# Attention scores in blocks of 128 queries of one expert, on two halves of TensorE's rows

## Chip, cores and metric

One core of a Trainium2 chip runs the whole kernel. The metric is the device time of one execution in microseconds, median of three runs.

## The reference

A linear attention feeds a mixture of experts with ordinary causal attention (batch B = 8, S = 576 positions, eight heads or 512 features, E = 4 experts of width 64, the best two of four per position). Cut to the second part, in which the change lies:

```python
q = x @ wq[e]; k = x @ wk[e]; v = x @ wv[e]        # for each expert e
scores = scale * (q @ k.transpose(0, 2, 1))
scores = np.where(causal, -1000000000.0, scores)
scores = scores - scores.max(-1, keepdims=True)
a = np.exp(scores)
a /= a.sum(-1, keepdims=True) + 1e-09
ye = a @ v @ wo[e]
...
out += mask[..., None] * w[:, :, kk:kk + 1] * ye
```

## The kernel before, in words

The linear attention runs over 32 pairs of heads: K and Q projections, features, sums over keys, numerator and denominator. Four pairs make the input x of one batch. For each of the eight batches the experts are taken in two groups g of two experts, and a group passes through these steps:

- `proj_t`: Q and K of both experts, transposed (64 dims of one expert on rows 0 to 63, of the other on rows 64 to 127). Values are held as a high and a low F32R part; a product is three matmuls (high by high, high by low, low by high).
- `scores(g)`: nine blocks i of 64 queries. `evac_q` lays Q out as block diagonals of 128 x 128, so that one matmul over all 128 rows gives 64 queries of the one expert on PSUM rows 0 to 63 and the same queries of the other below. Block i sees 64 (i + 1) keys; block 8 is cut into 256 and 320. That makes 10 PSUM tiles and 30 matmuls.
- `soft`: for each tile DVE adds the causal mask to the last 64 columns and takes the row maximum, ACT takes the exponential into `a` with its row sum, and the tile is free.
- `stream_t`: DVE turns the row sums into factors with the gates, DVE or ACT scales the nine blocks of `a`, PE transposes 25 pieces of 128 x 128 in seven PSUM tiles, and `evac_t` copies them into `at`.
- `attend`: the product with V, then `evac_y`, and after the second group the output projection.

All PSUM is one pool of eight tiles of 128 x 512, shared by every step. A planner writes the program's order: each stream of steps has a position, and of the steps that could start within 100 ns of the earliest the one with the lowest position is put next, by a table of costs per instruction. `in_order` then fixes that order on each engine. A change of costs or of steps so moves instructions of other streams too, and decides which PSUM tile a step gets.

`half_mm` in the K and Q projections of the linear attention (L396) already places two matmuls of 64 rows on the two halves of the rows, in F32.

## Time and profile before

| | |
|---|---|
| median of 3 runs (lowest, highest) | 777.0 us (776.93, 779.72) |
| the profiled execution's own time, its span | 773.74 us, 771.6 us |
| PE, DVE, ACT, POOL busy | 95%, 67%, 62%, 27% of the span |
| mean granted TensorE clock | 0.989 |

Busy is the time in which an engine had at least one instruction in work; matmuls overlap one another, so the sum over groups is more than the busy time, and the pace of a run of matmuls is read from start to start in the timeline.

### The profile page before, as it was taken

The page shows a single profiled execution, that of the slowest core. Times are in us where ns is not written, and L with a number is a line of the kernel's source. Part 1 is how long each engine was busy: PE and PEld are TensorE (multiplying, and loading weights), DVE is VectorE, ACT ScalarE, POOL GpSimd, SP SyncE. Part 2 cuts the span into 40 slices and gives each one's busy share as a digit, 9 for nine tenths or more (in the row PEclk, how much of TensorE's full clock was granted, in tenths as well). Part 3 has the DMA queues.
Part 4 walks back from the last instruction along what each step waited for, and adds up shares of the span by engine and source line. Part 5 has one row for each costly group of instructions (what it writes and reads, how often), then busy time and mean ns, then how long its engine had stood idle before and what let it go on. Part 6 is the DMA issues. An engine that isn't in the chain of part 4 may idle for free.

```text
span 771.6 us, 17860 instructions
## 1 busy us (share of the span) xinstructions
PE 730.1 (95%) x6927; PEld 564.4 (73%) x6927; DVE 520.3 (67%) x1368; ACT 475.7 (62%) x1096; POOL 211.5 (27%) x208
## 2 busy tenths in 40 slices
PE   5979899889999899999999999999999999999997
PEld 4655567666788567977779767886678876887986
DVE  3986855796567766698558766578657785376572
ACT  2764655667567664768546756666666686476474
POOL 2533542132321334040350144213332343010000
PEclk9999999899999999999999999999999999999998
DMA  4442321102112022102121212120211211010011
GB/s 122 141 143 64 93 57 34 35 18 67 53 34 97 17 69 82 54 17 82 51 67 35 78 36 73 48 96 17 68 52 34 65 35 35 2 47 18 1 62 62
DMA packets 38756, 43.63 MB, mean 57 GB/s; under 512 B 19088, under 2 KB 21648, under 8 KB 38672
## 3 DMA queue, kind: packets, MB, share of 16 engines
q1 hardware_dynamic: 38672, 42.49, 18.5%
q8 instruction: 55, 0.90, 0.5%
q14 instruction: 29, 0.24, 0.1%
HBM read 32.58 MB, written 9.44 MB: 54 GB/s over the span
## 4 chain that ended last, share of the span: by engine, by line
PE 80%; DVE 9%; DMA 3%; issue 2%; ACT 2%; SPq 2%; POOL 1%; DVEq 0%; POOLq 0%; ACTq 0%
PE ps_c L225 39%; PE ps_c L543 8%; PE ps_c L396 7%; PE ps_c L798 6%; PE ps_c L449 6%; PE ps_c L829 6%; PE ps_c L534 4%; PE ps_c L457 4%; DVE a L788 3%; DMA v_in<-in_v_dram 2%; SPq L257 2%; PE ps_c L467 1%; POOL mx L505 1%; DVE sm L778 1%; DVE u L507 0%
## 5 line engine op out<-in xcount | busy, mean ns | idle before, releaser
L505 POOL PARTITION_ALL_REDUCE mx<-u x64 | 138.4, 2212 | 203.7 <-ACT u L234 163.5
L225 PE MATMUL ps_c<-xh,qk 128*128 128x320 f32 (+1 forms) x512 | 109.2, 300 | 0.0
L236 ACT ACTIVATE ek<-ek 128x1152 f32<-128x1152 f32 x64 | 74.7, 1167 | 20.9 <-DVE ek L431 20.4
L236 ACT ACTIVATE a<-ps_c,nm 128x256 f32<-128x256 f32 (+7 forms) x160 | 79.7, 503 | 12.6 <-DVE nm L682 4.4
L225 PEld LDWEIGHTS ps_c<-xh,qk 128*128 128x128 f32 x512 | 83.4, 188 | 3.8 <-issue 1.9
L575 POOL PARTITION_BROADCAST xf<-dr x32 | 28.3, 884 | 188.1 <-DMA dr<-dc 59.5
L798 PE MATMUL ps_c<-ident,a 128*128 128x128 f32 x400 | 61.0, 295 | 17.9 <-DVE a L788 11.9
L225 PE MATMUL ps_c<-xl,qk 128*128 128x256 f32 (+1 forms) x256 | 75.5, 295 | 0.5 <-DVE xl L229 0.5
L682 DVE TENSOR_REDUCE nm<-ps_c 128x1 f32<-128x256 f32 (+7 forms) x160 | 71.8, 457 | 4.9
L798 PEld LDWEIGHTS ps_c<-ident,a 128*128 128x128 f32 x400 | 46.7, 148 | 36.3 <-DVE a L788 13.8
L449 PE MATMUL ps_c<-ek,v_in 128*64 128x256 f32 x512 | 63.0, 388 | 8.7 <-DMA v_in<-in_v_dram 6.6
L507 DVE TENSOR_TENSOR u<-u,mx 128x576 f32<-128x576 f32 x64 | 62.8, 992 | 10.2 <-POOL mx L505 9.9
L236 ACT ACTIVATE mx<-u 128x576 f32<-128x576 f32 x64 | 43.8, 684 | 41.3 <-DVE u L507 41.2
L431 DVE TENSOR_TENSOR ek<-ps_c,pmax 128x512 f32<-128x512 f32 (+1 forms) x96 | 50.3, 549 | 16.5 <-PE ps_c L457 16.3
L225 PE MATMUL ps_c<-vg,xh 128*128 128x260 f32 (+1 forms) x320 | 60.6, 289 | 0.0
L428 DVE TENSOR_REDUCE pmax<-ps_c 128x4 f32<-128x512 f32 (+1 forms) x96 | 49.9, 548 | 14.2 <-PE ps_c L396 14.2
L234 ACT COPY at<-ps_c 128x512 f32<-128x512 f32 (+1 forms) x94 | 49.2, 571 | 16.4 <-PE ps_c L798 14.9
L449 PEld LDWEIGHTS ps_c<-ek,v_in 128*64 128x64 f32 x512 | 35.3, 137 | 29.3 <-issue 4.6
L225 PE MATMUL ps_c<-yh,wo 128*128 128x256 f32 (+1 forms) x256 | 52.1, 298 | 0.0
L225 PE MATMUL ps_c<-kkh,qbdh 128*128 128x256 f32 (+7 forms) x160 | 51.0, 319 | 0.6 <-ACT a L236 0.6
L225 PEld LDWEIGHTS ps_c<-vg,xh 128*128 128x128 f32 (+1 forms) x320 | 47.2, 178 | 3.5 <-issue 2.0
L225 PE MATMUL ps_c<-kkl,qbdh 128*128 128x256 f32 (+7 forms) x160 | 49.7, 311 | 0.0
(119 smaller groups left out, 1635.8 us busy)
## 6 DMA issues: line engine op xcount, KB each, us to landing
v_in<-in_v_dram SPq DMA_DIRECT2D x32, 320.0 KB, 3.0
q_in<-in_qt_dram SPq DMA_DIRECT2D x64, 144.0 KB, 2.9
out_dram<-ot SPq DMA_DIRECT2D x32, 288.0 KB, 2.1
k_in<-in_kt_dram SPq DMA_DIRECT2D x32, 160.0 KB, 2.9
k_in<-in_kt_dram SPq DMA_DIRECT2D x32, 128.0 KB, 2.9
dc<-dr SPq DMA_DIRECT2D x128, 2.2 KB, 1.9
ot<-in_wts_dram SPq DMA_DIRECT2D x5, 288.0 KB, 3.6
k_in<-in_kt_dram SPq DMA_DIRECT2D x32, 32.0 KB, 2.4
```

The source lines that it names most:

```text
L225: nc.tensor.matmul(o, a, b, start=start, stop=stop, skip_group_check=True)
L234: nc.scalar.copy(o, i)
L236: nc.scalar.activation(o, i, func, **kw)
L396: nc.tensor.matmul(o, a, b, start=True, stop=True, skip_group_check=True)
L428: dve(n * 128, [mk], [pk]).tensor_reduce(out=m[:, us], in_=src, axis=AX.X, op=ALU.max, apply_absolute_value=True)
L431: dve(n * 128, [f'ek{p % EKB}1'], [pk, mk]).tensor_tensor(out=ek2[p % EKB][:, 1, us, :], in0=src, in1=m[:, us].unsqueeze(2).to_broadcast([ ...
L449: nc.tensor.matmul(o[64 * h:64 * h + 64], v_in[:, 4 * h + t, :], ek[:, :, 4 * h + t, :], start=t == 0, stop=False, skip_group_check=True)
L505: nc.gpsimd.partition_all_reduce(M, U, 128, bass_isa.ReduceOp.absmax)
L507: dve(S, [uk], [mk]).tensor_tensor(out=U, in0=U, in1=M, op=ALU.subtract)
L543: nc.tensor.matmul(ps[64 * h:64 * h + 64, 0:n], kvi[:, c, 64 * h:64 * h + 64], P_[h][c][:, s0:s1], start=c == 0, stop=c == 1, skip_group_c ...
L682: dve(n, [('nm', g, c)], [pk]).tensor_reduce(out=nm[g][:, c:c + 1], in_=src, axis=AX.X, op=ALU.max, negate=True)
L798: nc.tensor.transpose(ps[:, k * 128:(k + 1) * 128], a_blk[i][:, j, :], ident)
```

## The change

Queries 0 to 511 are taken in four blocks of 128 queries of one expert. The two experts of a group form a pair of matmuls of 64 rows, one on each half of the rows, which write two PSUM tiles; product by product the pair alternates. Block 8, the last 64 queries, keeps the block diagonal of both experts. There are still ten tiles and 30 matmuls in a step, 24 of them of 64 rows. `evac_q` writes the first 512 queries straight (128 rows at once) and only the last 64 as diagonals. The mask of blocks 0 to 7 is 128 columns wide. The factors of the sums are made in two instructions, the first eight with the gates as they lie on DVE, the ninth with a copy that POOL makes. `at` is laid out by expert, and a PSUM tile of transposes takes the pieces that lie together there, first blocks 0, 2, 4 and 6. The planner's costs for F32 and F32R matmuls change as well (`RATE`, `LDW`); positions and order tables stay.

```diff
+RATE = 2.18
+LDW = 109.0
...
         elif a.dtype == F32R:
-            cost = max(n / 2.4, 107.0) + 2.5
+            cost = max(n / RATE, LDW) + 5
...
-    maskf = xf[:, 0:128]
-    nc.gpsimd.memset(maskf, 0.0)
-    nc.gpsimd.affine_select(out=maskf, in_=maskf, pattern=[[-1, 128]], compare_op=ALU.is_ge,
+    mask2 = sb("mask2", [128, 128])
+    nc.gpsimd.memset(mask2, 0.0)
...
-    a_sets = [[sb(f"a{x}{i}", [128, (i + 2) // 2, 128]) for i in range(NB)] for x in range(AB)]
-    at = sb("at", [128, 25, 128])
-    qbd2 = [[sb(f"qbd{p}{g}", [128, NB, 128], F32R) for p in "hl"] for g in range(QB)]
+    a_sets = [[sb(f"a{x}{c}", [128, c // 2 + 1, 128]) for c in range(9)] for x in range(AB)]
+    at = sb("at", [128, 2, NJ, S])
+
+    q2 = [[sb(f"q{p}{g}", [128, S - 64], F32R) for p in "hl"] for g in range(QB)]
+    qbd2 = [[sb(f"qbd{p}{g}", [128, 128], F32R) for p in "hl"] for g in range(QB)]
...
         def evac_q(g, s0, s1, pk, ps):
-            i0, i1 = s0 // 64, s1 // 64
-            for h in range(2):
-                r = slice(64 * h, 64 * h + 64)
-                src = ps[r, 0:s1 - s0].rearrange("p (i s) -> p i s", s=64)
-                hi, lo = (qbd2[g % QB][x][r, i0:i1, r] for x in range(2))
-                hk = ('qbdh', g, s0, h)
+            pieces = [(min(s1, 512) - s0, slice(0, 128), [t[:, s0:min(s1, 512)] for t in q2[g % QB]], 0, f'q{g % QB}')]
+            if s1 == S:
+                for e in range(2):
+                    r = slice(64 * e, 64 * e + 64)
+                    pieces.append((64, r, [t[r, r] for t in qbd2[g % QB]], 512 - s0, f'qbd{g % QB}'))
+            for k, (n, r, (hi, lo), o, key) in enumerate(pieces):
+                src, hk = ps[r, o:o + n], ('qhi', g, s0, k)
                 yield Step('ACT', [pk], hot=True)
-                act(s1 - s0, hi, src, [hk, f'qbd0{g % QB}'], [pk], scale=SCALE)
+                act(n, hi, src, [hk, f'{key}0'], [pk], scale=SCALE)
                 yield Step('DVE', [hk], hot=True)
-                dve(s1 - s0, [f'qbd1{g % QB}'], [hk, pk]).scalar_tensor_tensor(
+                dve(n, [f'{key}1'], [hk, pk]).scalar_tensor_tensor(
                     out=lo, in0=src, scalar=SCALE, in1=hi.bitcast(F32), op0=ALU.mult, op1=ALU.subtract)
             plan.release('c', (pk, ps))
...
-            for i in range(NB):
-                w = 64 * (i + 1)
-                for s0, s1 in ((0, w),) if i < 8 else PARTS:
-                    pk, ps = yield Step('PE', [f'qbd0{g % QB}', f'qbd1{g % QB}', f'kk0{g % QB}', f'kk1{g % QB}'], 'c', ready), pos[0] + SLOPE[2] * i / 9
-                    o = ps[:, 0:s1 - s0]
-                    for n, (q_, k_) in enumerate(((0, 0), (0, 1), (1, 0))):
-                        mm(o, qbd2[g % QB][q_][:, i, :], kk2[g % QB][k_][:, s0:s1], n == 0, n == 2, s1 - s0, pk,
-                           [f'qbd{q_}{g % QB}', f'kk{k_}{g % QB}'])
-                    plan.spawn(soft(g, i, s0, s1, pk, ps), pos[0])
+            Q, K, x = q2[g % QB], kk2[g % QB], g % QB
+            products = ((0, 0), (0, 1), (1, 0))
+            need = [f'q0{x}', f'q1{x}', f'kk0{x}', f'kk1{x}']
+            for i in range(4):
+
+                w = 128 * (i + 1)
+                t0 = yield Step('PE', need, 'c', ready), pos[0] + SLOPE[2] * i / 5
+                t1 = yield Step('PE', need, 'c'), pos[0] + SLOPE[2] * i / 5
+                for n, (q_, k_) in enumerate(products):
+                    for e, (pk, ps) in enumerate((t0, t1)):
+                        r = slice(64 * e, 64 * e + 64)
+                        plan.run('PE', max(w / RATE, LDW) / 2 + 8, [pk], need)
+                        nc.tensor.matmul(ps[:, 0:w], Q[q_][r, 128 * i:128 * i + 128], K[k_][r, 0:w],
+                                         start=n == 0, stop=n == 2, skip_group_check=True)
+                for e, (pk, ps) in enumerate((t0, t1)):
+                    plan.spawn(soft(g, 2 * i + e, 0, w, pk, ps), pos[0])
+            need = [f'qbd0{x}', f'qbd1{x}', f'kk0{x}', f'kk1{x}']
+            for s0, s1 in PARTS:
+                pk, ps = yield Step('PE', need, 'c', ready), pos[0] + SLOPE[2] * 4 / 5
+                for n, (q_, k_) in enumerate(products):
+                    mm(ps[:, 0:s1 - s0], qbd2[x][q_], K[k_][:, s0:s1], n == 0, n == 2, s1 - s0, pk, need)
+                plan.spawn(soft(g, 8, s0, s1, pk, ps), pos[0])
...
-            if s1 == 64 * (i + 1):
-                dve(64, [pk], []).tensor_tensor(out=ps[:, n - 64:n], in0=ps[:, n - 64:n], in1=mask, op=ALU.add)
+            if i < 8 or s1 == S:
+                m = mask2 if i < 8 else mask
+                d = m.free_size()
+                dve(d, [pk], []).tensor_tensor(out=ps[:, n - d:n], in0=ps[:, n - d:n], in1=m, op=ALU.add)
...
-        yield Step('DVE', ['lg'], pred=lambda: all(('v', b, j) in done for j in range(NJ)))
+        yield Step('DVE', ['lg'], pred=lambda: all(('v', b, j) in done for j in range(NJ)) and (not b or ('n', b - 1, 1) in done))
...
-        yield Step('POOL', [G], pred=has('n', b - 1, 1) if b else None)
-        for g in range(2):
+        yield Step('POOL', [G])
+        for e in range(2):
+            plan.run('POOL', 200, ['gb'], [G])
+            nc.gpsimd.tensor_copy(gb[64 * e:64 * e + 64, :], w[0:64, 4, e:4:2])
+        done.add(('gate', b))
+
+
+    def at_groups():
+        out = []
+        for j in (0, 1):
             for e in range(2):
-                for h in range(2):
-                    plan.run('POOL', 130, ['gb'], [G])
-                    nc.gpsimd.tensor_copy(gb[64 * e:64 * e + 64, g, h:NB:2],
-                                          w[64 * h:64 * h + 64, 0:5 - h, 2 * g + e])
-        done.add(('gate', b))
-
-    units = [(i, j) for j in range(NJ) for i in range(2 * j, NB)]
+                out.append(([(2 * i + e, j) for i in range(j, 4)], [(0, 512 - 128 * j, at[:, e, j, 128 * j:512], None)]))
+        out.append(([(2 * i + e, 2) for e in range(2) for i in (2, 3)], [(0, 512, at[:, :, 2, 256:512], "p (e s) -> p e s")]))
+        out.append(([(8, j) for j in range(4)], [(0, 512, at[:, :, 0:4, 512:S].rearrange("p e j s -> p j e s"), "p (j e s) -> p j e s")]))
+        out.append(([(6, 3), (7, 3), (8, 4)], [(0, 256, at[:, :, 3, 384:512], "p (e s) -> p e s"),
+                                               (256, 128, at[:, :, 4, 512:S], "p (e s) -> p e s")]))
+        return out
+
+    groups = at_groups()
+    AT = [('at', k) for k in range(len(groups))]
...
-                dve(9, sk, ['gb']).tensor_tensor(out=s_, in0=s_, in1=gb[:, g, :], op=ALU.mult)
+                dve(8, sk, ['gate']).tensor_tensor(out=s_[:, 0:8].rearrange("p (i e) -> p i e", e=2),
+                                                   in0=s_[:, 0:8].rearrange("p (i e) -> p i e", e=2),
+                                                   in1=gt[:, 3, 0:4, 2 * g:2 * g + 2], op=ALU.mult)
+                dve(1, sk, ['gb']).tensor_tensor(out=s_[:, 8:9], in0=s_[:, 8:9], in1=gb[:, g:g + 1], op=ALU.mult)
                 done.add(('n', b, g))
                 for i in range(NB):
-                    w = 64 * (i + 1)
+                    w = 128 * (i // 2 + 1) if i < 8 else S
...
-                for u0 in range(0, 25, 4):
-                    n = min(4, 25 - u0)
-                    kc, ps = yield Step('PE', [('a', x, units[u0 + k][0]) for k in range(n)], 'c',
-                                        has('av', last // 2, last % 2) if last >= 0 else None), pos + SLOPE[3] * u0 / 25
-                    for k in range(n):
-                        i, j = units[u0 + k]
-                        plan.run('PE', 107, [kc], [('a', x, i)])
-                        nc.tensor.transpose(ps[:, k * 128:(k + 1) * 128], a_blk[i][:, j, :], ident)
-                    plan.spawn(evac_t(u0, n, kc, ps, last, b, g), pos)
+                for k, (slots, goes) in enumerate(groups):
+                    kc, ps = yield Step('PE', [('a', x, c) for c, j in slots], 'c',
+                                        has('av', last // 2, last % 2) if last >= 0 else None), pos + SLOPE[3] * k / 7
+                    for n, (c, j) in enumerate(slots):
+                        plan.run('PE', LDW + 5, [kc], [('a', x, c)])
+                        nc.tensor.transpose(ps[:, n * 128:(n + 1) * 128], a_blk[c][:, j, :], ident)
+                    plan.spawn(evac_t(k, goes, kc, ps, b, g), pos)
...
-    def evac_t(u0, n, kc, ps, last, b, g):
-        src = ps[:, 0:n * 128].rearrange("p (u c) -> p u c", c=128)
-        st = Step(copies(n * 128), [kc], hot=True)
+    def evac_t(k, goes, kc, ps, b, g):
+        st = Step(copies(sum(n for _, n, _, _ in goes)), [kc], hot=True)
         yield st
-        copy(st.eng, n * 128, at[:, u0:u0 + n, :], src, [('at', u0)], [kc])
+        for o, n, dst, shape in goes:
+            src = ps[:, o:o + n]
+            if shape:
+                src = src.rearrange(shape, **({'e': 2, 's': 64} if 'j' in shape else {'e': 2}))
+            copy(st.eng, n, dst, src, [('at', k)], [kc])
...
-        for i0_, i1 in ((0, 4), (4, 9)):
-            ak = [('at', x) for x in range(0, 25, 4)]
-            pk, ps = yield Step('PE', ak, 'c', ready), pos + SLOPE[3]
-            js = range(0, i1 // 2 + i1 % 2)
+                    and all(('at', b, g, k) in done for k in range(len(groups))))
+
+        for s0, s1 in PARTS:
+            pk, ps = yield Step('PE', AT, 'c', ready), pos + SLOPE[3]
+            js = range(0, (s1 + 127) // 128)
             for j in js:
                 kn = min(128, S - 128 * j)
-                i0 = max(i0_, 2 * j)
-                o, n = jbase(j) + i0 - 2 * j, 64 * (i1 - i0)
+                q0 = max(s0, 128 * j)
                 for e in range(2):
-                    plan.run('PE', 2 * n / 2.4 + 27, [pk], [f'vs{j}'] + ak)
-                    nc.tensor.matmul(ps[64 * e:64 * e + 64, 64 * (i0 - i0_):64 * (i1 - i0_)].rearrange("p (i s) -> p i s", s=64),
-                                     vs[j][:kn, g, e, :], at[:kn, o:o + i1 - i0, 64 * e:64 * e + 64],
+                    plan.run('PE', 2 * (s1 - q0) / RATE + 5, [pk], [f'vs{j}'] + AT)
+                    nc.tensor.matmul(ps[64 * e:64 * e + 64, q0 - s0:s1 - s0], vs[j][:kn, g, e, :], at[:kn, e, j, q0:s1],
                                      start=j == 0, stop=j == js[-1], skip_group_check=True)
-            plan.spawn(evac_y(b, g, 64 * i0_, 64 * i1, pk, ps), pos)
+            plan.spawn(evac_y(b, g, s0, s1, pk, ps), pos)
```

On PE, second group of the second batch (index 1), first matmul of each tile or block, before; `ps_c_61` to `ps_c_68` are the eight PSUM tiles, `qbdh` the high part of the block diagonals, the last number the keys:

```order
L225 MATMUL ps_c_66<-kkh_151,qbdh_149 128x64
...
L225 MATMUL ps_c_64<-kkh_151,qbdh_149 128x128
...
L225 MATMUL ps_c_68<-kkh_151,qbdh_149 128x192
...
L225 MATMUL ps_c_63<-kkh_151,qbdh_149 128x256
...
L225 MATMUL ps_c_62<-kkh_151,qbdh_149 128x320
...
L225 MATMUL ps_c_67<-kkh_151,qbdh_149 128x384
...
L225 MATMUL ps_c_65<-kkh_151,qbdh_149 128x448
...
L225 MATMUL ps_c_61<-kkh_151,qbdh_149 128x512
...
L225 MATMUL ps_c_66<-kkh_151,qbdh_149 128x256
...
L225 MATMUL ps_c_64<-kkh_151,qbdh_149 128x320
```

The same place now; the two rows of a width are the two experts, `qh` is the high part of the queries laid out straight:

```order
L671 MATMUL ps_c_66<-kkh_154,qh_150 128x128
L671 MATMUL ps_c_68<-kkh_154,qh_150 128x128
...
L671 MATMUL ps_c_65<-kkh_154,qh_150 128x256
L671 MATMUL ps_c_67<-kkh_154,qh_150 128x256
...
L671 MATMUL ps_c_61<-kkh_154,qh_150 128x384
L671 MATMUL ps_c_66<-kkh_154,qh_150 128x384
...
L671 MATMUL ps_c_68<-kkh_154,qh_150 128x512
L671 MATMUL ps_c_65<-kkh_154,qh_150 128x512
...
L219 MATMUL ps_c_67<-kkh_154,qbdh_152 128x256
...
L219 MATMUL ps_c_61<-kkh_154,qbdh_152 128x320
```

Before, a tile of this step (66) comes back at the ninth tile; now 66 comes back at the sixth, and the 512-wide pair and block 8 take 68, 65, 67 and 61, the second to fifth, once more.

On PE a little later, where the transposes of this group begin, before (`ek` by `ones` are sums over keys of the linear attention, `a_139` to `a_147` the nine blocks of exponentials, `mx` by `kv` numerators):

```order
L457 MATMUL ps_c_68<-ek_100,ones 32x128 x16
L457 MATMUL ps_c_68<-ek_100,sel 32x128 x4
L798 MATMUL ps_c_66<-ident,a_139 128x128
L798 MATMUL ps_c_66<-ident,a_140 128x128
L798 MATMUL ps_c_66<-ident,a_141 128x128
L798 MATMUL ps_c_66<-ident,a_142 128x128
...
L543 MATMUL ps_c_67<-mx_123,kv_110 64x256
L543 MATMUL ps_c_67<-mx_124,kv_110 64x256
```

The same place now (`a_140` to `a_148` are the nine blocks, the last rows ahead of the transposes denominators):

```order
L452 MATMUL ps_c_65<-ek_101,ones 32x128 x16
L452 MATMUL ps_c_65<-ek_101,sel 32x128 x4
L538 MATMUL ps_c_66<-mx_124,kv_111 64x256
L538 MATMUL ps_c_66<-mx_125,kv_111 64x256
...
L529 MATMUL ps_c_68<-mx_121,kv_110 32x320
L529 MATMUL ps_c_68<-u_115,kv_110 32x320
L820 MATMUL ps_c_62<-ident,a_140 128x128
L820 MATMUL ps_c_62<-ident,a_142 128x128
L820 MATMUL ps_c_62<-ident,a_144 128x128
L820 MATMUL ps_c_62<-ident,a_146 128x128
```

Numerators and denominators now stand ahead of the transposes, not among them, and the first tile of transposes takes blocks 0, 2, 4, 6 where it took 0, 1, 2, 3.

On DVE, first group of the fourth batch (index 3), between the last copy of the gates' logits (`lg`) and softmax, before (`ge`, `gt`, `gs` belong to the gates, `nm` is the maximum):

```order
L568 RECIPROCAL dc_127<-dc_127 128x9
L652 COPY lg<-ps_c_64 64x4
L735 TENSOR_TENSOR ge<-lg 128x80
...
L744 TENSOR_TENSOR gt<-lg,gs 128x20
L681 TENSOR_TENSOR ps_c_65<-ps_c_65,mask 128x64
L682 TENSOR_REDUCE nm_163<-ps_c_65 128x1
L681 TENSOR_TENSOR ps_c_63<-ps_c_63,mask 128x64
```

The same place now:

```order
L692 TENSOR_TENSOR ps_c_68<-ps_c_68,mask_77 128x128
L693 TENSOR_REDUCE nm_166<-ps_c_68 128x1
...
L693 TENSOR_REDUCE nm_166<-ps_c_63 128x1
L692 TENSOR_TENSOR ps_c_64<-ps_c_64,mask 128x64
L693 TENSOR_REDUCE nm_166<-ps_c_64 128x1
...
L648 COPY lg<-ps_c_65 64x4
...
L746 TENSOR_TENSOR ge<-lg 128x80
L748 TENSOR_TENSOR ge<-ge,tri 128x80
```

The eight instructions of the gates stood ahead of the masks; now they stand behind all masks and maxima of the step, and so does the last copy of `lg`.

## Rows read from the trace of the kernel before

**Rows 1.** The page, parts 1 and 4: engines, and the chain by engine.

```profile
PE 730.1 (95%) x6927; PEld 564.4 (73%) x6927; DVE 520.3 (67%) x1368; ACT 475.7 (62%) x1096; POOL 211.5 (27%) x208
...
PE 80%; DVE 9%; DMA 3%; issue 2%; ACT 2%; SPq 2%; POOL 1%; DVEq 0%; POOLq 0%; ACTq 0%
```

**Rows 2.** Waits of PE over the span: us in total, times, longest us.

```profile
PE ps_c L798 <- DVE a L788: 11.9, 15, 2.3
```

**Rows 3.** Timeline of PE in one scores step: start us, us, what.

```profile
432.32 0.28 PE L225 MATMUL ps_c<-kkh,qbdh 128*128 128x64 f32 x1
...
432.65 0.31 PE L225 MATMUL ps_c<-kkh,qbdh 128*128 128x128 f32 x1
...
434.20 0.34 PE L225 MATMUL ps_c<-kkh,qbdh 128*128 128x384 f32 x1
...
434.74 0.37 PE L225 MATMUL ps_c<-kkh,qbdh 128*128 128x448 f32 x1
...
435.35 0.40 PE L225 MATMUL ps_c<-kkh,qbdh 128*128 128x512 f32 x1
...
436.06 0.27 PE L225 MATMUL ps_c<-kkh,qbdh 128*128 128x256 f32 x1
...
436.94 3.07 PE L829 MATMUL ps_c<-at,vs 128*64 128x256 f32 x28
```

**Rows 4.** Timeline of DVE over the same stretch.

```profile
433.14 0.23 DVE L681 TENSOR_TENSOR ps_c<-ps_c,mask 128x64 f32<-128x64 f32 x1
...
433.54 0.22 DVE L681 TENSOR_TENSOR ps_c<-ps_c,mask 128x64 f32<-128x64 f32 x1
...
434.54 0.22 DVE L681 TENSOR_TENSOR ps_c<-ps_c,mask 128x64 f32<-128x64 f32 x1
...
435.14 0.22 DVE L681 TENSOR_TENSOR ps_c<-ps_c,mask 128x64 f32<-128x64 f32 x1
...
443.24 5.23 DVE L788 TENSOR_SCALAR a<-a,sm 128x64 f32<-128x64 f32 x6
```

**Rows 5.** Timeline of ACT over the same stretch.

```profile
433.87 0.19 ACT L236 ACTIVATION_READ_ACCUMULATOR a<-ps_c,nm 128x1 f32 x1
...
435.63 0.19 ACT L236 ACTIVATION_READ_ACCUMULATOR a<-ps_c,nm 128x1 f32 x1
```

**Rows 6.** Chain that ended last, in order of time, 380 to 440 us.

```profile
381.38 2.09 PE ps_c L543 x16
383.47 1.11 PE ps_c L534 x16
...
394.36 1.09 PE ps_c L396 x16
395.45 0.42 PE ps_c L225 x2
```

**Rows 7.** Timeline of PE where a K projection begins.

```profile
393.84 0.40 PE L225 MATMUL ps_c<-vg,xh 128*128 128x260 f32 x2
394.08 0.28 PE L225 MATMUL ps_c<-vg,xl 128*128 128x260 f32 x1
394.29 1.16 PE L396 MATMUL ps_c<-wf,k_in 64*128 64x128 f32 x16
```

**Rows 8.** Groups on DVE, shapes apart: xcount | busy us, mean ns | idle.

```profile
L681 DVE TENSOR_TENSOR ps_c<-ps_c,mask 128x64 f32<-128x64 f32 x144 | 32.1, 223 | 0.7 <-PE ps_c L225 0.4 <-ACT at L234 0.4
...
L431 DVE TENSOR_TENSOR ek<-ps_c,pmax 128x128 f32<-128x128 f32 x32 | 9.1, 284 | 0.1
...
L775 DVE TENSOR_TENSOR sm<-sm 128x1 f32<-128x1 f32 x16 | 5.3, 330 | 0.9 <-ACT a L236 0.9
```

**Rows 9.** Timeline of PE at one group of transposes; in brackets idle time, releaser.

```profile
262.76 0.52 PE L798 MATMUL ps_c<-ident,a 128*128 128x128 f32 x3 [1.28 <-DVE a L788]
263.72 0.44 PE L798 MATMUL ps_c<-ident,a 128*128 128x128 f32 x2 [0.44 <-DVE a L788]
264.74 2.41 PE L798 MATMUL ps_c<-ident,a 128*128 128x128 f32 x11 [0.58 <-DVE a L788]
```

More of the change, by code (lines that the diff above doesn't have):

```diff
@@ L48 @@
 NPAIRS = B * NP
+RATE = 2.18
+LDW = 109.0
 PSUM_TILES = (("c", 8, 512),)
-def jbase(j):
-    return 10 * j - j * j
 def at_batch(b):
     return NP * b + BOFF[b]
-def abase(i):
-    return sum((ii + 2) // 2 for ii in range(i))
 class Step:
@@ L218, in mm @@
         if a.dtype == F32:
-            cost = max(n * 4 / 2.4, 214.0) + 2.5
+            cost = max(n * 4 / RATE, 2 * LDW) + 5
         elif a.dtype == F32R:
-            cost = max(n / 2.4, 107.0) + 2.5
+            cost = max(n / RATE, LDW) + 5
         else:
@@ L271, in tile_linear_attn_moe @@
         r_ = slice(64 * h, 64 * h + 64)
-        nc.vector.tensor_copy(mask[r_, :], maskf[r_, r_])
+        nc.vector.tensor_copy(mask[r_, :], mask2[r_, r_])
     tri = sb("tri", [128, 4, 4])
@@ L360, in zeros @@
         for x in range(AB):
-            for i in range(0, NB, 2):
-                yield Step('POOL')
-                plan.run('POOL', 88, [('a', x, i)])
-                nc.gpsimd.memset(a_sets[x][i][:, i // 2, 64:128], 0.0)
+            yield Step('POOL')
+            plan.run('POOL', 88, [('a', x, 8)])
+            nc.gpsimd.memset(a_sets[x][8][:, 4, 64:128], 0.0)
         done.add(('w', 4))
@@ L393, in half_mm @@
     def half_mm(o, a, b, n, w, r):
-        plan.run('PE', 2 * n / 2.4 + 20, [w], r)
+        plan.run('PE', 2 * n / RATE + 8, [w], r)
         nc.tensor.matmul(o, a, b, start=True, stop=True, skip_group_check=True)
@@ L532, in stream_n @@
                         g = 64 * h + 32 * c
[L533 removed]
+                        plan.run('PE', n / RATE + 5, [pk], Pk + [kvk])
                         nc.tensor.matmul(ps[g:g + 32, 0:n], kvi[:, 2, g:g + 32], P_[h][c][:, s0:s1],
```

13 lines of the change are left out of this document (6 added, 7 removed).

## The prediction

> **What bounds the kernel now.** I read the page first: PE is busy 95% of the span, DVE 67%, ACT 62%, POOL 27%, and in the chain that ended last PE holds 80% of the time and DVE 9% [rows 1]. So PE's own work is the bound nearly everywhere, and an instruction taken off PE counts in full wherever PE does not run into a wait sooner. The list of PE's waits says where it does wait: above all at the transposes, for a block of exponentials that DVE has just scaled, 15 times and 11.9 us in all [rows 2]. The timeline of one scores step then gives the spacing of its matmuls, which follow one another without a gap [rows 3], and DVE's and ACT's timelines of the same step show how far softmax runs behind it [rows 4, 5].
>
> **What the change does to PE.** From one start to the next, a step takes 436.94 − 432.32 = 4.62 us: three matmuls 64 keys wide take 0.33 (0.11 each, the pace at which full-height weights follow one another), three 384 wide 0.54, three 512 wide 0.71, and block 8 with its 256 + 320 keys 0.88 [rows 3]. Afterwards blocks 0 to 7 are four pairs (128, 256, 384, 512 keys), three products each; block 8 stays as it is. Whether a pair costs one matmul or two rests on rows of the K projection, which already puts two 64-row F32 matmuls on the two halves of the rows: its 16 records, eight pairs, take 1.09 us, 0.136 a pair, while two full-height F32 records of the same 128x128 shape take 0.42, 0.21 each [rows 6]. Two halves cost less than one whole, so they do run side by side. A 64-row pair of F32R is in no row. Its lower bound is the single matmul (0.11, 0.11, 0.18, 0.237), its upper bound twice that; I take 0.136 for the two narrow widths, by the nearest row, and the single price for 384 and 512, where the stream is longer than that pace. Entering half-height work costs something: from the last full-height matmul to the first K projection pass 0.21 us where 0.12 is usual for those 260 columns [rows 7], so 0.09, twice a step (in, and out again before block 8). The step is then 0.09 + 0.41 + 0.41 + 0.54 + 0.71 + 0.09 + 0.88 = 3.13 us. It saves 1.49 us, and 16 steps save **23.8 us**. Bounds: 26.2 us with pairs at the single price, and a loss of 4.5 us with no overlap.
>
> **What takes part of it back: PSUM tiles.** A pair takes two tiles at once, and a tile returns only after mask, maximum and exponential. In rows: DVE's first mask starts 0.82 us after the step's first matmul, and ACT is done with that first tile at 433.87 + 0.19 = 434.06, 0.92 after the mask; for the 256-wide tile it is 435.63 + 0.19 − 434.54 = 1.28 [rows 3 to 5]. DVE goes from mask to mask in 0.40 us (64 wide) to 0.60 (256 wide) [rows 4], that is about 1.04 ns a column, and a 128-wide mask costs some 0.06 more than a 64-wide one (284 against 223 ns) [rows 8]. With the new widths I get masks at 0.82, 1.36, 1.90, 2.57, 3.24 and returns (1.1, 1.1, 1.35, 1.35, 1.6 later) at 1.9, 2.5, 3.25, 3.9, 4.8 us for tiles 1 to 5. What PE waits for is set by the order: before, a step first takes up one of its own tiles again at its eighth or ninth; in the changed order I counted nine steps that do so at the ninth tile, one at the eighth, three at the seventh and three at the sixth (the step shown in the section on the change is one of the last). By the step's own starts (pairs at 0.1, 0.5, 0.9, 1.45, block 8 at 2.25 and 2.6):
> - ninth: tiles 1 and 2 are back in time, the work behind waits 0.1 us. Net gain 1.37.
> - eighth: 0.76 us of waits, net gain 0.73.
> - seventh: the 512 pair waits 1.0, block 8 0.3, what follows 0.4. Net loss 0.2.
> - sixth: half of the 384 pair waits 1.0, the 512 pair 0.8, block 8 and what follows 0.7. Net loss 1.0.
>
> The sum is 9 × 1.37 + 0.73 − 0.7 − 3.1 = 9.3 us of gain left; the waits cost **14.5 us**. Queued behind a waiting pair on PE are block 8 and then the second group's projections or the product with V, and DVE and ACT wait for these. Bounds: nothing if tiles return sooner, all of the 23.8 if DVE is often late.
>
> The Trainium skill's page "TensorEngine Tiling (Array Packing)", section Performance Considerations, says under PSUM Bottleneck that tiling speeds up TensorE but not the emptying of PSUM, so that the copy out may become the bottleneck. By that rule the gain ends where DVE's pace begins; no row of before shows it yet, since PE's scores steps run without a gap.
>
> **What moves on DVE and ACT.** For a group, eight masks grow (0.5 us), the maxima read 256 more columns (0.27), and the scaling of the sums is two instructions instead of one (0.33 [rows 8]): softmax ends **1.1 us later** after a step's start. Four Q copies with their four remainders become narrower, which gives DVE and ACT about as much back outside that path; the row-parts of `at` are copied in eight pieces for seven. Instructions by the order: DVE 1370 before and 1355 now, ACT 938 and 985. Five per cent on ACT's 62% does not make it the bound, so I cost these at nothing; their cover is the third of the span in which each is idle. Without it, DVE's 1.1 us a group would be 17.6 us. POOL loses six of eight small copies per batch and has 73% idle. The gates no longer stand ahead of the masks on DVE in any batch, which is why 0.82 is good for all steps.
>
> **The transposes.** The first group of four used to need blocks 0 to 3; now it needs 0, 2, 4 and 6, three scalings later. Six scalings on DVE (with three on ACT) took 5.23 us [rows 4], 0.58 a block: 1.7 us later, with the 1.1 above 2.8. Behind the waiting transposes stand numerator and denominator matmuls in PE's queue, and for these the division waits. Now in batches 0 and 1 those two pieces, 2.09 + 1.11 = 3.2 us [rows 6], stand ahead of the second group's transposes: where PE waited 1.28 + 0.44 + 0.58 = 2.3 us [rows 9], 2.3 + 2.8 − 3.2 = 1.9 is left, 0.4 less, twice. In batch 4 only the numerators are ahead: 2.8 − 2.1 = 0.7 more. In batch 3 it is a K projection (1.5 us): 1.3 more. At the end of the last batch nothing is left to cover the longer softmax: +1.1. Together **+2.3 us**.
>
> **Sum.** −23.8 + 14.5 + 2.3 = −7.0 us. The profiled execution's own time is 773.7 us (span 771.6), so it becomes 766.7. The median of the runs is 777.0, 3.3 above it; I keep that distance: **770 us**.
>
> **The rivals.**
> - *No waits for tiles.* PE takes all of it: 777 − 23.8 + 2.3 = 755.5. For it speaks that the steps of before never stall; against it that DVE takes 0.5 to 0.8 us a tile, where PE would issue ten of them in 3.
> - *The weights of a pair load one after the other*, at the 0.11 pace of the narrow matmuls [rows 3]: pairs at 0.22, 0.22, 0.22, 0.237. The step is 3.75 and saves 0.87, 13.9 in all; slower pairs wait less (0.8 at the seventh, 1.6 at the sixth, 7.2 together). 777 − 13.9 + 7.2 + 2.3 = 772.6. The K projection's 0.136 speaks against it.
> - *The waits eat everything*, DVE being late at most steps: 777 + 2.3 = 779, no change.
> - *The change doesn't do what it says*: F32R halves run in turn. 777 + 4.5 + 2.3 = 784. Only that the rows are of F32 speaks for it.
> - *Slower, by the transposes.* If the pieces moved ahead don't cover (a numerator waits for the broadcast on POOL), the 2.8 us fall due in each batch's second group: 777 − 9.3 + 8 × 2.8 = 790. It decides from 9.3 / 2.8, four groups on. For it: PE already waits there 15 times [rows 2]; against it: work was put in front.
>
> The Trainium skill's page "TensorE: Matmul & The Clock Gate", section on LDWEIGHTS, gives loading time by the weight's columns alone, half height costing as much as full; by that, estimated from the page, two loads of 128 columns in series take 213 ns, the second rival's price. The trace's 136 ns a pair disagrees with series loading, for F32.
>
> **How the numbers follow.** About 0.5% (3.9 us) is what a measurement here can tell from no change. Chances: my forecast 0.50 (760 to 773) and loads in series 0.08, no tile waits 0.08, waits eat all 0.17, halves in turn 0.05, transposes 0.12. Faster (below 773.1) is the first three, 0.66; same 0.17; slower 0.17. The range from 755 to 783 takes in the tile waits from almost none to all; it leaves out some 0.04 below and 0.14 above.
>
> **What the profile would show.** Right: a scores step of 24 half-height matmuls with pairs starting within some ns of each other, about 3 us where the tiles are there; PE waits for ACT's exponentials inside the steps that come back to a tile early, some 10 to 15 us in all; PE busy near 707 us; DVE near 520. Wrong: spacing of a 512 pair near 0.47 us (halves in turn); no idle time in the steps (755); idle time before the transposes well above 12 us with less work in front (slower).

## The result, and the profile after

The changed kernel takes **752.9 us** (median of 4 runs, 752.1 to 754.8); the kernel before took 777.0 in the same session. The ratio is 0.969, 95% interval 0.966 to 0.973: 24 us faster, where 7 were forecast, 2 us below the range. The profiled execution took 754.8 us (span 753.0).

The page, parts 1 and 4, for the lines of [rows 1]; then the waits of PE over the span (us in total, times, longest us) for [rows 2]:

```profile
PE 714.3 (95%) x6948; PEld 541.0 (72%) x6948; DVE 497.5 (66%) x1353; ACT 477.2 (63%) x1143; POOL 201.4 (27%) x156
...
PE 77%; DVE 11%; ACT 6%; issue 3%; DMA 2%; POOL 1%; SPq 0%; DVEq 0%; ACTq 0%; POOLq 0%
```

```profile
PE ps_c L820 <- DVE a L812: 8.6, 6, 4.2
PE ps_c L671 <- ACT a L230: 5.3, 11, 0.9
PE ps_c L444 <- DMA v_in<-in_v_dram: 3.7, 2, 2.5
PE ps_c L462 <- DVE kvt L240: 2.9, 2, 2.1
PE ps_c L671 <- DVE at L240: 1.6, 1, 1.6
```

All transposes of exponentials, before and now (x count | busy us, mean ns | PE's idle time before them, and what ended it):

```profile
L798 PE MATMUL ps_c<-ident,a 128*128 128x128 f32 x400 | 61.0, 295 | 17.9 <-DVE a L788 11.9 <-ACT a L236 5.2
L820 PE MATMUL ps_c<-ident,a 128*128 128x128 f32 x400 | 55.9, 292 | 9.6 <-DVE a L812 8.6 <-ACT a L230 0.5 <-DVE at L240 0.5
```

PE's busy time fell by 15.8 us (730.1 to 714.3). What it stands idle (span less busy) is 38.7 against 41.5, but at other places: the idle time before transposes went from 17.9 to 9.6 us, and a new kind stands beside it, waits *inside* the scores steps (L671; 8.4 us with those of block 8), where a pair wants a PSUM tile that, mostly, ACT has not yet emptied.

PE's timeline of a scores step without such a wait (start us, us), for [rows 3]:

```profile
673.81 0.33 PE L671 MATMUL ps_c<-kkh,qh 64*128 64x128 f32 x2
673.98 0.28 PE L671 MATMUL ps_c<-kkl,qh 64*128 64x128 f32 x2
674.09 0.27 PE L671 MATMUL ps_c<-kkh,ql 64*128 64x128 f32 x2
674.20 0.33 PE L671 MATMUL ps_c<-kkh,qh 64*128 64x256 f32 x2
...
674.49 0.28 PE L671 MATMUL ps_c<-kkh,ql 64*128 64x256 f32 x2
674.61 0.34 PE L671 MATMUL ps_c<-kkh,qh 64*128 64x384 f32 x2
...
675.13 0.39 PE L671 MATMUL ps_c<-kkh,qh 64*128 64x512 f32 x2
675.36 0.40 PE L671 MATMUL ps_c<-kkl,qh 64*128 64x512 f32 x2
...
675.92 0.39 PE L219 MATMUL ps_c<-kkh,qbdh 128*128 128x256 f32 x1
...
676.94 0.39 PE L219 MATMUL ps_c<-yh,wo 128*128 128x256 f32 x1
```

Each row with x2 is a pair. The three 128-wide pairs take 0.39 us, a 512-wide pair 0.23, as long as one matmul of that width before: the halves do run side by side. The step takes 3.13 us. Now one that comes back to a tile early, and the granted clock (PEclk, the last column but two) of the two steps and of a part of the second:

```profile
242.54 0.44 PE L671 MATMUL ps_c<-kkh,qh 64*128 64x384 f32 x1
243.44 0.44 PE L671 MATMUL ps_c<-kkh,qh 64*128 64x384 f32 x1 [0.46 <-ACT a L230]
...
244.74 0.59 PE L671 MATMUL ps_c<-kkh,qh 64*128 64x512 f32 x1 [0.27 <-ACT a L230]
```

```profile
core 0: us, PE busy (x) PEld busy (x) DVE busy (x) ACT busy (x) POOL busy (x), PEclk, DMA share, GB/s
673.81:676.94 3.13, 3.13 (x32) 2.50 (x31) 2.34 (x9) 2.30 (x9) 0.00 (x0) 1.00 0.08 8
241.68:247.86 6.18, 5.46 (x32) 3.70 (x31) 5.40 (x17) 4.69 (x16) 0.00 (x0) 0.77 0.03 2
245.00:248.40 3.40, 3.40 (x15) 2.13 (x15) 3.30 (x8) 2.47 (x8) 0.00 (x0) 0.50 0.00 0
```

The second matmul of a pair starts 0.90 us after its twin, because its tile comes late, and the step takes 6.18 us. The idle time marked is only a part of that: some of a wait shows as wide spacing, and from 245.00 us on PE was granted half its clock (0.50, the 1.2 GHz level) for 3.4 us. Two of the 16 steps have such a stretch; another, at 593.55 us, stood idle for 1.88 us in all and kept the full clock.

### The profile page after: what moved, and what is told of

It reads as the page before. It is cut to its first block, busy times and chain, and to the rows that moved or that the text cites. A ratio compares the mean times of both kernels' runs of the same rounds, so it can differ in the third digit from the quotient of the medians.

```text
span 753.0 us, 17887 instructions
## 1 busy us (share of the span) xinstructions
PE 714.3 (95%) x6948; PEld 541.0 (72%) x6948; DVE 497.5 (66%) x1353; ACT 477.2 (63%) x1143; POOL 201.4 (27%) x156
## 4 chain that ended last, share of the span: by engine, by line
PE 77%; DVE 11%; ACT 6%; issue 3%; DMA 2%; POOL 1%; SPq 0%; DVEq 0%; ACTq 0%; POOLq 0%
PE ps_c L219 30%; PE ps_c L391 8%; PE ps_c L538 8%; PE ps_c L444 8%; PE ps_c L820 5%; PE ps_c L452 5%; PE ps_c L852 5%; PE ps_c L529 4%; DVE nm L693 3%; ACT a L230 3%; DVE ps_c L692 2%; PE ps_c L671 2%; PE ps_c L462 2%; DMA v_in<-in_v_dram 2%; ACT ek L230 1%
## 5 line engine op out<-in xcount | busy, mean ns | idle before, releaser
L500 POOL PARTITION_ALL_REDUCE mx<-u x64 | 140.6, 2239 | 189.0 <-ACT u L228 184.0
L230 ACT ACTIVATE a<-ps_c,nm 128x256 f32<-128x256 f32 (+4 forms) x160 | 83.1, 523 | 21.2 <-DVE nm L693 14.1
L693 DVE TENSOR_REDUCE nm<-ps_c 128x1 f32<-128x256 f32 (+4 forms) x160 | 76.1, 484 | 4.9
L502 DVE TENSOR_TENSOR u<-u,mx 128x576 f32<-128x576 f32 x64 | 60.6, 950 | 7.2 <-POOL mx L500 6.8
L820 PE MATMUL ps_c<-ident,a 128*128 128x128 f32 x400 | 55.9, 292 | 9.6 <-DVE a L812 8.6
L228 ACT COPY at<-ps_c 128x512 f32<-128x512 f32 (+3 forms) x109 | 47.9, 522 | 8.3 <-PE ps_c L820 7.5
L228 ACT COPY u<-ps_c 128x320 f32<-128x320 f32 (+1 forms) x120 | 39.9, 412 | 17.2 <-PE ps_c L391 16.0
L852 PE MATMUL ps_c<-at,vs 128*64 128x320 f32 (+4 forms) x448 | 50.0, 366 | 0.6 <-ACT a L230 0.4
```

Of the source, the lines that this page charges most:

```text
L228: nc.scalar.copy(o, i)
L230: nc.scalar.activation(o, i, func, **kw)
L500: nc.gpsimd.partition_all_reduce(M, U, 128, bass_isa.ReduceOp.absmax)
L502: dve(S, [uk], [mk]).tensor_tensor(out=U, in0=U, in1=M, op=ALU.subtract)
L693: dve(n, [('nm', g, c)], [pk]).tensor_reduce(out=nm[g][:, c:c + 1], in_=src, axis=AX.X, op=ALU.max, negate=True)
L820: nc.tensor.transpose(ps[:, n * 128:(n + 1) * 128], a_blk[c][:, j, :], ident)
```

## The experiments

Eighteen kernels, each timed in 3 rounds beside the kernel before (777.4 to 777.9 in these sessions). Span and busy time are of the profiled execution; *rest* is span less PE's busy time, that is waits, and some 13 us before the first and behind the last matmul. The four kernels that leave out a part of the computation are told of in the text alone.

| kernel | scores | us | ratio to before, 95% | span | PE busy | rest |
|---|---|---|---|---|---|---|
| before | old | 777.0 | 1 | 771.6 | 730.1 | 41.5 |
| e1 new costs | old | 749.4 | 0.960 to 0.965 | 747.9 | 722.0 | 25.9 |
| e6 costs halfway | old | 770.2 | 0.986 to 0.993 | 768.9 | 730.5 | 38.4 |
| e7 new costs, full-height only | old | 745.8 | 0.956 to 0.962 | 743.4 | 720.4 | 23.0 |
| e9 old costs, output held | old | 766.9 | 0.983 to 0.990 | 765.2 | 729.7 | 35.5 |
| e13 old costs x 1.01 | old | 772.0 | 0.990 to 0.995 | 770.6 | 731.9 | 38.7 |
| e15 costs of e7 x 1.01 | old | 749.7 | 0.960 to 0.969 | 747.6 | 722.2 | 25.4 |
| **the change** | new | 752.9 | 0.966 to 0.973 | 753.0 | 714.3 | 38.7 |
| e2 old costs | new | 763.4 | 0.978 to 0.984 | 759.8 | 714.5 | 45.3 |
| e5 even blocks scaled first | new | 753.9 | 0.965 to 0.972 | 753.4 | 714.3 | 39.1 |
| e8 pairs charged double | new | 756.4 | 0.970 to 0.977 | 754.9 | 714.0 | 40.9 |
| e10 output held | new | 764.1 | 0.979 to 0.987 | 763.0 | 720.8 | 42.2 |
| e11 output held, last batch | new | 752.2 | 0.964 to 0.973 | 749.3 | 712.1 | 37.2 |
| e12 as e5 and e10 | new | 751.2 | 0.963 to 0.970 | 748.7 | 712.7 | 36.0 |
| e14 costs x 1.01 | new | 765.1 | 0.980 to 0.990 | 762.2 | 719.9 | 42.3 |
| e16 costs of e7, pairs double | new | 757.6 | 0.970 to 0.981 | 755.3 | 713.7 | 41.6 |

**Costs or scores?** The change replaces the planner's costs too. e1 is the kernel before with these alone, e2 the change with the old ones.

```diff
 # e1, in the kernel before (and likewise the half-height costs); e2 is the reverse, in the change
-            cost = max(n / 2.4, 107.0) + 2.5
+            cost = max(n / RATE, LDW) + 5
```

> The scores of before, with the planner's costs for F32 and F32R matmuls taken from the change (RATE, LDW and what hangs on them); the instructions are those of before in another order. Theory A, that most of the gain comes from the new costs through the order of all the other work: 758 to 764 us. Theory B, that it comes from the shorter scores step and its lighter softmax, with whatever order: 774 to 780 us, no change. In between, 765 to 773, both have a share.

> The whole change but for the costs: the planner counts F32 and F32R matmuls as before, and a pair as half of max(keys / 2.4, 107) + 8 each. Theory A (costs and order): about 770 us, since the 16 scores steps alone took only 5 us less in the two profiles. Theory B (the shorter step): 751 to 758 us, as the change.

The costs alone give 28 us, more than the whole change; the scores with the old costs give 14. e1 is below both of its theories, e2 between its two. The two don't add: to the new costs the new scores bring 3.6 us *more* time (752.9 less 749.4), which is no more than the draws below. The waits of PE in e7, the fastest kernel, show what the order does: the 15 waits for scaled exponentials of [rows 2], 11.9 us, are gone, and PE is busy 10 us less too, in part because less of that is at half clock (mean granted clock 0.997, before 0.989).

```profile
PE ps_c L225 <- DVE identb L263: 8.8, 1, 8.8
PE ps_c L449 <- DMA v_in<-in_v_dram: 6.4, 4, 4.8
PE ps_c L467 <- POOL mx L505: 1.4, 1, 1.4
PE ps_c L467 <- ACT kvt L234: 0.8, 1, 0.8
PE ps_c L225 <- ACT a L236: 0.7, 2, 0.4
PE ps_c L798 <- ACT a L236: 0.7, 3, 0.3
```

**Nearness of the costs, or a draw?** Two tables between the old and the new one, then three kernels whose PE costs are only multiplied by 1.01.

```diff
 # e6: RATE = 2.3, LDW = 107 in e1.   e7: new costs in mm() alone.   e13, e14, e15:
+            cost *= 1.01        # for PE, in Plan.run
```

> The kernel before with its scores unchanged and a planner's cost table that lies between the old one and the new one: 2.3 columns a ns and 107 ns for weights instead of 2.18 and 109 (the old table divides by 2.4). Theory A1 (the new costs are nearer to what the trace shows, and the time falls with the distance to them): between 777 and 749, that is 757 to 769. Theory A2 (any shift of the costs throws the order about, and the order of before was merely a bad one): anywhere from 745 to 780, with no relation to the costs; under 752 or over 774 would speak for it.

> The kernel before with its scores unchanged and the new costs only for the full-height F32 and F32R matmuls (projections, scores, V, output); the half-height and quarter-height ones of the linear attention and of the product with V keep their old, higher costs. Theory A1 (accuracy of the costs): 750 to 758, since the costs that are changed cover most of PE's time. Theory A2 (any other order will do): anywhere from 745 to 780. The sum of waits on PE, 28.9 us between first and last matmul in the kernel before, is expected to move with the time, while matmul time at full clock stays within 3 us of 713.

> The kernel before with its scores and its cost table, every PE cost multiplied by 1.01 in the planner. Nothing else. Theory A1 (the costs' nearness to the durations makes the order good): one per cent is a tenth or less of what the new table moves (2.4 to 2.18 columns a ns), so 773 to 779, within 4 us of the kernel before. Theory A2 (a draw among orders): a change of over 4 us in either direction, by waits and half clock, with matmul time at full clock within 3 us.

> The change with every PE cost multiplied by 1.01 in the planner, nothing else. Theory A1: 750 to 756, within 4 us of the change (752.9). Theory A2: over 4 us away in either direction; then the change's own gain is known only to the width of such draws.

> The kernel before with the new costs for full-height matmuls alone (745.8 us), every PE cost multiplied by 1.01 in the planner. Theory A1: 743 to 749. By the built order the work between scores and transposes stays as large as it was there (second groups 9.7 to 28.5 us of matmuls, the last 8.1), so waits before transposes should stay near 1 us if that cover is what counts. Theory A2: over 4 us away, upwards, since 745.8 is the best draw so far.

Neither theory holds alone. One per cent on the costs moves the time by 5.5, 12 and 4 us, so there is a draw, and the change's 752.9 is a good one: e14, with the same scores, is no faster than e2 with the old costs (765.1 and 763.4). That the new costs help the *new* scores is therefore not shown beyond a draw. But the draws lie in groups: old scores with old costs 772 and 777, halfway 770, with the new costs 746, 749 and 750. That the new costs make a better order for the old scores is shown; that nearness to the true durations is why was only argued (e7 takes half of the new table back, and was the fastest).

**The halves, and DVE's share.** e3 puts both matmuls of a pair on the same rows (it leaves out the second expert's scores, computing the first's twice); e4 leaves out the causal mask on DVE. Both keep the change's order.

```diff
-                        r = slice(64 * e, 64 * e + 64)
+                        r = slice(0, 64)
 # e4
-                dve(d, [pk], []).tensor_tensor(out=ps[:, n - d:n], in0=ps[:, n - d:n], in1=m, op=ALU.add)
+                dve(d, [pk], [])
```

> The change, with both matmuls of a pair on rows 0 to 63, so that the second expert's scores are those of the first (that part of the result is left out); order, tiles and all other work stay. If the two halves really run side by side, a step without waits grows from 3.1 to about 4.8 us, the steps that wait for tiles by less: 8 to 20 us in all, 761 to 773 us. If a pair ran in turn all along: 753, no change.

> The change without the causal mask's additions (128 x 128 wide and 16 x 64 wide instructions on DVE left out, so the scores are not causal); order and tiles stay. If PE's waits inside the scores steps are set by DVE's pace, tiles return 0.33 us sooner each: a step that comes back to a tile early falls from 5.4 to about 4.3 us, and with the earlier end of softmax the whole falls by 6 to 15 us, 738 to 747 us. If the waits only move on to the next wait (transposes, or ACT's exponentials), 750 to 753 us.

e3 took 771.15 us (762.4 to 772.9; ratio 0.980 to 0.994): by the medians running side by side is worth 18 us under this order, though one run of e3 is only 9.5 us above the change. In its trace a 512-wide pair takes 0.47 us (666.83 to 667.30) where the change takes 0.23. e4 took 742.1 (0.950 to 0.956): 11 us hang on 39 us of DVE's busy time (497.5 to 458.1), though DVE is busy only 66% of the span.

**Where the order puts work.** In e1 and e7 one to four pieces of the output projection stand between the second scores step of a batch and its transposes, in every batch but the first; in the kernel before none do in five of the eight. e9, e10 and e11 hold them there by hand, and e5, e8 and e12 try to take the tile waits away.

```diff
 # e9 in the kernel before, e10 in the change; e11 in the change with b == 6 alone
+                late = b in (0, 1, 2, 3, 4, 5, 6) and 2 * t + (s0 > 0) >= 5
-                pk, ps = yield Step('PE', yk, 'c', has('w', 3)), ...
+                pk, ps = yield Step('PE', yk, 'c', has('s', b + 1, 1) if late else has('w', 3)), ...
 # e5; e12 is e5 and e10 together
-                for i in range(NB):
+                for i in (0, 2, 4, 6, 1, 3, 5, 7, 8):
 # e8
-                        plan.run('PE', max(w / RATE, LDW) / 2 + 8, [pk], need)
+                        plan.run('PE', max(w / RATE, LDW) + 5, [pk], need)
```

> The kernel before with its scores and its costs unchanged; alone the last three of the eight output-projection pieces of a batch (18 of 48 matmuls) are held until the second scores step of the next batch has been issued, so that they stand between these scores and their transposes. Theory E (what the new costs gained is cover: work that PE has left between the second scores step of a batch and its transposes): in the kernel before these gaps hold 5.7 to 8.1 us of matmuls in batches 0, 1, 3, 4 and 7, and PE waits 2 to 2.5 us there with up to 3.4 us at half clock behind it; all of that goes, some 11 us of waits and 3 of clock: 757 to 765. Theory F (the new costs gain by something else, the loads of v or the order of the linear attention): the same waits move elsewhere, 770 to 778.

> The whole change with the same hold of 18 output-projection matmuls per batch. Theory E: idle time of PE before transposes falls from 9.6 to about 5 us, the half-clock stretch behind the last batch's 4.2 us wait goes too (some 3 us): 742 to 747 against 752.9. The waits for tiles inside the scores steps stay (8.4 us), since seven steps still take a tile up again at the sixth or seventh. Theory F: 751 to 755.

> The whole change with 18 output-projection matmuls held in the last batch alone; all other places of the order are as in the change. Theory E: the wait of 4.2 us before the last transposes and 6.2 us at half clock behind it (3 us lost) go, at no price elsewhere: 746 to 749. Theory F: the work held is only done later, 752 to 755.

> The change, with the nine scalings of a block of exponentials in the order 0, 2, 4, 6, 1, 3, 5, 7, 8 instead of 0 to 8, so that the first transposes (blocks 0, 2, 4, 6) have what they need after four scalings and not seven. It also moves the order: four scores steps instead of seven take a PSUM tile up again before the ninth. Theory A (what is left of the scores' gain is lost in waits for tiles, and in the order around them): the waits inside the scores steps fall from 8.4 us to about 4, those before the transposes from 9.6 to about 5; time 744 to 749 against 752.9 for the change. Theory C (waits before transposes do not hang on the order of the scalings, PE being held by the softmax as a whole): 751 to 755.

> The change, with the planner charging a pair's matmuls at the full price of a full-height one each (as if the halves went in series), so that it believes a scores step to last as long as before. By the built order four steps instead of seven take a tile up before the ninth. Theory A (waits for tiles are what the order of the change costs): waits inside the scores steps fall from 8.4 us to 3 to 6, time 745 to 750. Theory D (the planner misplaces what follows by as much as it is wrong, so that waits only move to transposes and projections): 752 to 760.

> The whole change with both edits: the hold of 18 output-projection matmuls in each batch, and scalings in the order 0, 2, 4, 6, 1, 3, 5, 7, 8, whose order has four early steps in place of seven. Theory E: waits inside the scores steps 4.8 us as in the run with the scalings alone, waits before transposes down from 13.4 to about 5: 740 to 745, below all kernels so far. Theory F: 752 to 756, as with the scalings alone.

e9 gains 10.5 us, less than forecast: cover for the transposes is one part of what the new costs bring, not all. In the change the same hold *costs* 11 us (e10), and in the last batch alone it gives nothing (e11); why e10 loses was not settled. e5 and e8 changed one wait for another: by the traces e5 cut the idle time inside the scores steps from 8.4 to 4.8 us, and that before the transposes rose from 9.6 to 13.4. e12, with e5's edit and e10's together, took 751.2, outside both of its ranges, though e10's alone cost 11: as most of these edits also move the rest of the order, differences of a few us among them show little. None of the eight other kernels with the new scores that keep all the work is below 751.

**The shorter step under the best order.** e16 gives the change e7's costs, with a pair's matmuls charged at the full price each; its order then has, in most batches, as much work behind a scores step as e7's.

> The change with the cost table of the fastest kernel so far (new costs for full-height matmuls alone) and a pair's matmuls charged at the full price each. By the built order no step takes a tile up before the eighth (three at the eighth, thirteen at the ninth), and the work between scores and transposes is as large as in the fastest kernel. If the shorter step and the order add: matmul time 18 us below 718, waits 5 to 10 us above the 10.5 of the fastest kernel: 735 to 742. If the shorter step only uncovers the softmax (theory D): idle time rises to 25 us and more, 748 to 756, as in the run with pairs charged double.

It took 757.6 us against 745.8: they don't add. Three stretches show why, from the first matmul of a scores step to the last of its transposes: the first step of batches 6 and 7 and the second of batch 7, with the same kinds and counts of matmuls between. First e7, then e16 (columns as in the windows above):

```profile
645.80:666.78 20.98, 20.98 (x167) 18.59 (x165) 16.88 (x59) 15.05 (x44) 3.20 (x10) 1.00 0.08 29
698.51:716.10 17.59, 17.59 (x134) 17.18 (x133) 15.45 (x54) 12.32 (x37) 1.49 (x8) 1.00 0.09 35
716.13:729.92 13.79, 13.64 (x103) 11.26 (x102) 10.10 (x34) 11.51 (x34) 0.00 (x0) 1.00 0.12 44
```

```profile
656.90:678.06 21.16, 19.78 (x166) 16.87 (x165) 18.06 (x61) 14.19 (x44) 2.07 (x4) 1.00 0.08 29
710.03:727.75 17.72, 16.29 (x133) 15.43 (x133) 15.22 (x54) 11.94 (x38) 0.36 (x2) 1.00 0.09 35
727.96:741.78 13.82, 12.15 (x102) 9.54 (x101) 11.77 (x37) 11.31 (x33) 0.00 (x0) 1.00 0.12 44
```

PE's busy time is 1.20, 1.30 and 1.49 us less with the new scores, and the stretches are 0.18, 0.13 and 0.03 us *longer*. In the third, nearly all of PE's idle time in e16 is waits for scaled exponentials:

```profile
PE ps_c L820 <- DVE a L812: 1.6, 2, 1.3
```

In the first two the wait is in the scores step, 1.3 us for a tile. There DVE works through the eight gate instructions ahead of the first mask (L692), which so starts 2.3 us after the step's first matmul. In the change, where no gates stand ahead of the masks, as the prediction said, it starts after 0.6 us (the last line, from the step at 652.37 us):

```profile
657.59 0.24 DVE L746 TENSOR_TENSOR ge<-lg 128x80 f32<-128x80 f32 x1
...
659.13 0.18 DVE L755 TENSOR_TENSOR gt<-lg,gs 128x20 f32<-128x20 f32 x1
659.22 0.29 DVE L692 TENSOR_TENSOR ps_c<-ps_c,mask 128x128 f32<-128x128 f32 x1
```

```profile
652.95 0.30 DVE L692 TENSOR_TENSOR ps_c<-ps_c,mask 128x128 f32<-128x128 f32 x1
```

In e16 it is so in six of the 16 steps, which have 9.1 of the 12.6 us that PE stands idle inside the steps; e7 has the gates there too, but its longer steps wait 0.8 us in all. So what DVE does around the softmax, gates included, seems to set the length with the new scores, while PE's own work filled it with the old ones. No run moves the gates alone, so their share in e16's loss is open. If DVE sets the length, less work on DVE must shorten e16 and not e7: e17 and e18 are e7 and e16 without the causal mask, as e4 leaves it out, their order unchanged.

> The fastest kernel so far (old scores, new costs for full-height matmuls alone, 745.8 us) without DVE's additions of the causal mask; the order of everything else is the same. It leaves out the masking. About 35 us of DVE's work go (144 masks 64 wide, at 0.223 us each 32 us). Theory D (PE waits for the softmax only where its own work between scores and transposes is short, and here it is long enough): PE's idle time before scores and transposes is 1.9 us in all, so at most 3 us fall: 742.5 to 746. Theory G (DVE's load as a whole slows the kernel): 735 to 740.

> The change under the order of the fastest kernel (757.6 us) without DVE's additions of the causal mask; the order is the same, and the masking is left out. Theory D (the shorter step uncovers the softmax, which DVE paces): PE's idle time inside scores steps (12.6 us) and before transposes (7.7) falls by more than half, 10 to 16 us in all: 741 to 748. Theory G: as much as in the run beside it, and no more. Theory H (the change loses to something else than the softmax): 754 to 758.

e17 took 745.9 us (0.958 to 0.961), as e7 did; e18 took 741.6 (0.950 to 0.955), 16 us less than e16. So the shorter step loses 12 us to the old one with the masks (757.6 against 745.8) and gains 4 without them (741.6 against 745.9). The 12 and the 4 compare two orders, and so hold to the width of a draw; the 0 and the 16 for the masks don't, since e17 keeps e7's order and e18 that of e16. The same three stretches, first in e17, then in e18:

```profile
647.08:667.90 20.82, 20.82 (x167) 18.57 (x166) 15.08 (x50) 14.66 (x44) 3.22 (x10) 1.00 0.08 30
699.62:716.94 17.32, 17.32 (x134) 17.13 (x133) 13.65 (x45) 11.82 (x37) 1.50 (x8) 1.00 0.09 35
716.97:730.76 13.79, 13.64 (x103) 11.25 (x102) 8.57 (x25) 11.23 (x34) 0.00 (x0) 1.00 0.12 44
```

```profile
645.76:666.14 20.38, 19.41 (x165) 16.86 (x165) 15.72 (x52) 13.67 (x44) 2.08 (x4) 1.00 0.08 30
696.58:713.46 16.88, 15.90 (x134) 15.42 (x133) 12.75 (x45) 11.86 (x38) 0.36 (x2) 1.00 0.10 36
713.66:726.59 12.93, 11.95 (x102) 9.49 (x101) 9.31 (x28) 10.36 (x32) 0.00 (x0) 1.00 0.12 47
```

In e18 they are 0.8 to 0.9 us shorter than in e16, in e17 only 0 to 0.3 shorter than in e7. Where the time went was forecast less well: the rest fell by 4.5 us only (41.6 to 37.1) and PE's busy time by 10.7. The 16 scores steps, by their starts, fell by 6.9 us, of which 1.7 is marked as idle; a late tile also shows as wide spacing and half clock. With the new scores DVE's work, the masks in it, paces PE in these stretches; with the old ones it doesn't. It is not DVE alone: 2.3 to 2.5 us of DVE's busy time left each stretch of e18, and the waits for tiles are on ACT's exponentials, whose share no run takes apart. This is the rule that the prediction quoted from the Trainium skill, "TensorEngine Tiling (Array Packing)", Performance Considerations, PSUM Bottleneck: here, where softmax empties the tiles, the trace agrees, with 16 us for the masks in one kernel and 0 in the other.

## Why the prediction was wrong

The step that failed is the one on the order. The prediction read it where tiles and transposes need it and then summed "−23.8 + 14.5 + 2.3"; the new table of planner costs, which moves every piece of work on PE, had **no term**. e1 measures it alone, on the old scores, at −28 us, more than the result. With the old table the new scores take 763.4 us (e2), inside the 760 to 773 of the forecast; the last 10.5 us, to 752.9, came with the new table, and are of the size of one draw. The forecast's own parts, point by point:

- *PE bounds the kernel*: right; PE holds 77% of the chain, before 80%.
- *The step of 3.13 us, halves side by side*: right. Five steps without a wait take 3.06 to 3.13 us. The pairs were priced at 0.136 for the narrow widths; the three 128-wide ones took 0.39 in all, 0.13 each with the entry. That the total agrees to a hundredth is in part luck: the 128-wide pairs with the entry took 0.11 less than forecast, and what stands from the 512-wide pairs to the step's end 0.13 more (675.13 to 676.94, 1.81 for 1.68). e3 excludes the rival of halves in turn.
- *Tile waits, 14.5 us*: right in kind, 5 us too small. By the starts of their first matmul and of the work behind (less 32 matmuls of other work that stand in one of them), the 16 steps take 69.4 us and would take 49.6 at 3.1: **19.8 us**. Before they took 74.4, so the steps gained 5.0 us where the sum had 9.3. Missing was the half clock, as at 245 us: by the granted clock of the two steps that have it (0.77 and 0.75) some 3 us, an estimate.
- *DVE costed at nothing, "DVE near 520"*: wrong twice. DVE is busy 497.5 us; either half of the change alone brings most of the fall from 520.3 (e7, costs, 499.6; e2, scores, 503.6). And softmax is not covered: e4 and e18 show 11 and 16 us hanging on the masks, a part of which is the tile waits that the sum did price.
- *Transposes, +2.3 us*: wrong in sign over all. Idle time ahead of them fell from 17.9 to 9.6 us; with the old costs (e2) it is 15.6, so most of the fall is the new table's order. Of the single places, the end of the last batch was right in kind, 4.2 us of wait in place of 2.3; the sum entered +1.1 there, without the 1.7 us of later scalings that it had just worked out.
- *The rivals*: 755.5, "no waits for tiles", is nearest in time and wrong in its mechanism; the waits are there, and the order paid for them. The premise of the sum, one order for both, is met by no pair of kernels; the nearest is e2 against the kernel before, −14 us.

With a term for the order, −28, the sum would have said 742, now 11 too low; that the two parts share the same slack fits this, and e16 to e18 bear it out for one order, one with the gates ahead of the masks. How far any such sum can be trusted is what e13 and e14 show, 5 to 12 us for costs that differ by one per cent.

## What to carry to other kernels

When a change touches a planner's costs, run the old program with the new costs first: that was worth 28 us, and the fastest full kernel here, e7 at 745.8 us (0.956 to 0.962 of before), has the old scores. Before shortening a step on the busiest engine, take the stretch from its start to where its result is needed and ask what else sets that length: where PE had been busy throughout, 1.2 to 1.5 us saved on it came back as 1.4 to 1.5 us of idle time. And test the width of the draw (costs times 1.01) before a few per cent are put down to a cause.
